# A gated linear attention and its MLP on one core: another order for the first phase, and products of gates with q and k taken from PSUM

## The chip, the core and the metric

One core of a Trainium2 chip. It has TensorE for matrix products (its loading of weights is listed as PEld), VectorE (DVE), ScalarE (ACT), GpSimd (POOL) and SyncE (SP), each with its own in-order instruction stream, on-chip memories SBUF and PSUM of 128 partitions, and DMA queues to HBM. TensorE writes to PSUM, and its results are read from there by VectorE and ScalarE. The metric is the device time of one execution in microseconds (us); lower is better.

## The reference

```python
# q, k, v, f_logit: (4, 8, 768, 48) float32
f = 1.0 / (1.0 + np.exp(-f_logit))
for t in range(S):                       # S = 768
    state = f[:, :, t, :, None] * state + np.einsum('bhd,bhe->bhde', k[:, :, t], v[:, :, t])
    y[:, :, t] = np.einsum('bhd,bhde->bhe', q[:, :, t], state)
x = y.transpose(0, 2, 1, 3).reshape(4, 768, 384)
mu, var = mean and variance of x over its last axis
xn = (x - mu) / np.sqrt(var + 1e-06) * g_ln
out = x + np.maximum(xn @ w_ch1, 0.0) @ w_ch2      # w_ch1 384 x 1536, w_ch2 1536 x 384
```

The two weight matrices arrive as 64-bit floats, which the kernel reads as pairs of 32-bit integers (`words`: `low` and `high`) and turns into 32-bit floats itself.

## The kernel before

**Units.** The 768 time steps are cut into 12 units of 64 steps, each for all four batches and eight heads (256 rows of the MLP). `attention(n)` (line 491) is a generator of four stages. Stage 1: `across` transposes the gates `f` on TensorE into single PSUM banks (tiles `tr`), ScalarE's sigmoid writes them to SBUF, and two scans on VectorE form the products of gates `after` (from each step to the unit's end) and `upto` (from the start), with small operations between them (`total`, its reciprocal, `least`). Stage 2: `k` and `q` are transposed, copied by ScalarE to `zk` and `zq` (line 531), and multiplied on POOL with `after` and `upto` to `kh` and `qh` (lines 534, 535). Stage 3: `kept` is the state times `total`; TensorE makes `py` from `qh` and `kept`, the scores `ps` from `kh` and `qh`, and `kp`, the transpose of `kh`; VectorE masks the scores (`sc`). Stage 4: `py` gets the scores' product with `v`; `pn` is the unit's contribution to the state, which VectorE adds; ScalarE copies `py` to `x`; mean and variance follow (`bn_stats`, `bn_aggr`, then `rstd` on POOL).

**MLP.** `normalize(n)` and `turn(n)` make `xn` and its transpose `xt` (tile `xp` in PSUM). `mlp(n)` (line 632) has 12 parts, each ending in a yield. Six are of `ph`: two of twelve strips of the hidden layer, from `xt` and `w1`, with ScalarE's ReLU into `h`. Six are of `po`: for each of two row groups three parts of four strips from `h` and `w2`, then VectorE's add `o` and two output DMAs. The matmul records of the trace count each 32-bit product twice, so a `ph` part has 12 and a `po` part 8 records.

**PSUM.** `ps1` (line 358) has four single banks, used in turn by `tr`, `kp`, `xp`, `ph` and `po`; `ps2` has two pairs for `py`, `ps` and `pn`.

**Order.** `manual_schedule` keeps the instructions of each engine in program order, and the program's order is written out in the last loops. Before the main loop three attentions run, with steps of the conversion of w1 between their stages; then the rest of w1, then `normalize(0)` and `turn(0)`. In the main loop the parts of `mlp(m)` alternate with the stages of `attention(m + 3)`, and in the first round three steps of the conversion of w2 follow each part.

**Conversion.** `weights` (line 421) takes each matrix in six pieces of 128 x 768 numbers, fetched one piece ahead. A piece goes through VectorE (exponent), POOL twice (limits, shift), VectorE (sign; fraction's bits), ScalarE (fraction to float), VectorE (low word), and a last product, on VectorE for w1, where the gain `g_ln` is multiplied in, on POOL for w2. Each step waits for the one before.

**Loads.** `load(n)` issues 16 DMAs of 96 KB on SyncE's queue, four for each of `f`, `q`, `k` and `v`. The tiles of `f`, `q` and `k` exist twice and are used in turn.

Of the kernel before, what the change touches and what calls it, by code (L numbers as in the profile page):

```python
# [8 lines left out]
FP32 = mybir.dt.float32  # L9
# [8 lines left out]
def general_path(tc, q, k, v, f_logit, w1, w2, ident, out):  # L18
# [228 lines left out]
    def mlp(n):  # L247
# [17 lines left out]
        for c in range(2):  # L265
            pt = one_bank(f"gxp{n}")[:, 0:KD * C].rearrange("p (m t) -> p m t", m=KD)
            for m in range(KD):
                nc.tensor.transpose(pt[:, m], xn[:, c, m * P:(m + 1) * P], ident)
            nc.scalar.copy(out=xt[:, :, c * C:(c + 1) * C], in_=pt)
# [33 lines left out]
def kernel(  # L303
# [38 lines left out]
    AHEAD = 3  # L342
# [4 lines left out]
    w2 = outer.tile([P, KF, DM], FP32)  # L347
    small = outer.tile([1, 1], I32)
# [5 lines left out]
    stage = fast.enter_context(tc.tile_pool(name="stage", bufs=2))  # L354
    work = fast.enter_context(tc.tile_pool(name="work", bufs=1))
    xs = fast.enter_context(tc.tile_pool(name="xs", bufs=AHEAD + 2))
# [20 lines left out]
    def load(n):  # L377
        if n >= NU:
            return
        vt = raws.tile([P, G, H, D], FP32, tag="rawv", name=f"v{n}")  # L380
        loaded[n] = [wide_heads[name, n % 2] for name in "fqk"] + [vt]
        for t, src in zip(loaded[n], (f_logit, q, k, v), strict=True):
            for b in range(B):
                nc.sync.dma_start(  # L384
                    out=t[(b % 2) * T:(b % 2 + 1) * T, b // 2, :, 0:D],
                    in_=src[b, :, n * T:(n + 1) * T, :].rearrange("h p d -> p h d"))

    load(0)
# [11 lines left out]
    nc.vector.memset(power, -0.5)  # L400

# [4 lines left out]
    for i in range(2):  # L406
        t = consts.tile([P, NS, E1], FP32, name=f"starts{i}")
        nc.vector.memset(t, 0.0)
        starts.append(t)
        t = consts.tile([P, NS * E1 + 1], FP32, name=f"gates{i}")  # L410
        nc.gpsimd.memset(t, 0.0)
        gates.append(t)
# [4 lines left out]
    gain = consts.tile([P, KD], FP32)  # L417
# [3 lines left out]
    def weights(dst, src, name, scaled):  # L421
        rows, cols = dst.shape[1], dst.shape[2]
        sv = src.rearrange("(c p) f -> p c f", p=P)
        r, w = (rows, PIECE // rows) if scaled else (PIECE // cols, cols)
        pieces = [(slice(i, i + r), slice(j, j + w))
                  for i in range(0, rows, r) for j in range(0, cols, w)]
        wide = src.dtype == mybir.dt.int64
        staged = []
        if wide:
            def fetch(i):  # L430
                ci, fi = pieces[i]
                words = stage.tile([P, r, 2 * w], I32, tag="words", name=f"{name}words{i}")
                nc.sync.dma_start(out=words, in_=sv[:, ci, fi].bitcast(I32))
                staged.append(words)
        else:
            def fetch(i):
                ci, fi = pieces[i]
                nc.sync.dma_start(out=dst[:, ci, fi], in_=sv[:, ci, fi])
        fetch(0)
        for i, (ci, fi) in enumerate(pieces):  # L440
            if i + 1 < len(pieces):
                fetch(i + 1)
            to = dst[:, ci, fi]
            if not wide:
                for c in range(r if scaled else 0):
                    nc.vector.tensor_scalar_mul(out=to[:, c], in0=to[:, c],
                                                scalar1=gain[:, c:c + 1])
                yield
                continue
            words = staged.pop(0)  # L450
            scale = stage.tile([P, r, w], I32, tag="scale", name=f"{name}scale{i}")
            frac = stage.tile([P, r, w], FP32, tag="frac", name=f"{name}frac{i}")
            wv = words.rearrange("p r (f two) -> p two r f", two=2)
            low, high = wv[:, 0].bitcast(U32), wv[:, 1]


            nc.vector.tensor_scalar(out=scale, in0=high, scalar1=20, scalar2=0x7FF,
                                    op0=ALU.logical_shift_right, op1=ALU.bitwise_and)
            nc.gpsimd.tensor_scalar(out=scale, in0=scale, scalar1=float(BIAS + 255),
                                    scalar2=float(BIAS), op0=ALU.min, op1=ALU.max)  # L460
            nc.gpsimd.tensor_scalar(out=scale, in0=scale, scalar1=float(-BIAS),
                                    scalar2=float(1 << 23), op0=ALU.add, op1=ALU.mult)
            yield
            nc.vector.scalar_tensor_tensor(out=scale, in0=high, scalar=-(1 << 31), in1=scale,  # L464
                                           op0=ALU.bitwise_and, op1=ALU.bitwise_or)

            nc.vector.tensor_scalar(out=high, in0=high, scalar1=0xFFFFF, scalar2=None,  # L467
                                    op0=ALU.bitwise_and)
            nc.scalar.activation(out=frac, in_=high, func=AF.Copy, bias=1.0, scale=2.0 ** -20)
            yield  # L470
            nc.vector.scalar_tensor_tensor(out=frac, in0=low, scalar=2.0 ** -52, in1=frac,
                                           op0=ALU.mult, op1=ALU.add)
            if scaled:
                for c in range(r):
                    nc.vector.scalar_tensor_tensor(  # L475
                        out=to[:, c], in0=frac[:, c], scalar=gain[:, c:c + 1],
                        in1=scale[:, c].bitcast(FP32), op0=ALU.mult, op1=ALU.mult)
            else:
                nc.gpsimd.tensor_tensor(out=to, in0=frac, in1=scale.bitcast(FP32), op=ALU.mult)  # L479
            yield  # L480

    pairs = [(g, a) for g in range(G) for a in range(NP)]
    x_of, xn_of, xt_of = {}, {}, {}
# [7 lines left out]
    def attention(n):  # L491

        fr, qr, kr, vt = loaded.pop(n)
        gt, st = gates[n % 2], starts[n % 2]
        gv = gt[:, 0:NS * E1].rearrange("p (s e) -> p s e", e=E1)


        zq = work.tile([P, NS, T], FP32, tag="zq", name=f"zq{n}")
        zk = work.tile([P, NS, T], FP32, tag="zk", name=f"zk{n}")

        def across(src, g):
            pt = one_bank(f"tr{n}")
# [5 lines left out]

        for g in range(G):
            pt = across(fr, g)  # L510
            nc.scalar.activation(out=gv[:, g * 8:(g + 1) * 8, 1:E1], in_=pt, func=AF.Sigmoid)  # L511

        after = work.tile([P, NS, E1], FP32, tag="after", bufs=2, name=f"after{n}")
        nc.vector.tensor_tensor_scan(  # L514
            out=after.rearrange("p s e -> p (s e)")[:, ::-1], data0=gt[:, NS * E1:0:-1],
            data1=ends.rearrange("p s e -> p (s e)")[:, ::-1], initial=0.0,
            op0=ALU.mult, op1=ALU.add)
        total = work.tile([P, NS], FP32, tag="total", bufs=2, name=f"total{n}")
        nc.vector.tensor_scalar_max(out=total, in0=after[:, :, 0], scalar1=1e-30)
        nc.vector.reciprocal(out=st[:, :, 0], in_=total)  # L520
        nc.vector.tensor_tensor(out=least, in0=least, in1=total, op=ALU.min)

        upto = work.tile([P, NS, E1], FP32, tag="upto", name=f"upto{n}")
        nc.vector.tensor_tensor_scan(  # L524
            out=upto.rearrange("p s e -> p (s e)"), data0=gt[:, 0:NS * E1],
            data1=st.rearrange("p s e -> p (s e)"), initial=0.0, op0=ALU.mult, op1=ALU.add)
        yield
        for src, dst in ((kr, zk), (qr, zq)):
            for g in range(G):
                pt = across(src, g)  # L530
                nc.scalar.copy(out=dst[:, g * 8:(g + 1) * 8], in_=pt)  # L531
        kh = work.tile([P, NS, T], FP32, tag="kh", bufs=2, name=f"kh{n}")
        qh = work.tile([P, NS, T], FP32, tag="qh", bufs=2, name=f"qh{n}")
        nc.gpsimd.tensor_tensor(out=kh, in0=zk, in1=after[:, :, 1:E1], op=ALU.mult)  # L534
        nc.gpsimd.tensor_tensor(out=qh, in0=zq, in1=upto[:, :, 1:E1], op=ALU.mult)  # L535
# [11 lines left out]
        if n:  # L547
            for e, (g, a) in enumerate(pairs):
# [8 lines left out]
        for e, (g, a) in enumerate(pairs):  # L557
# [19 lines left out]
        for across_ in range(2):  # L577
            for e, (g, a) in enumerate(pairs):
                for b in range(2):
# [4 lines left out]
                                     skip_group_check=True)  # L584
        if n < NU - 1:
# [10 lines left out]
            else:  # L596
                nc.vector.tensor_copy(out=state, in_=pnv)
        x = xs.tile([P, G, DM], FP32, tag="x", name=f"x{n}")
        x_of[n] = x
        nc.scalar.copy(out=x.rearrange("t g (a r d) -> t r (g a) d", r=2, d=D),  # L600
                       in_=py[:, :, 0:GA * D].rearrange("t r (e d) -> t r e d", d=D))
        stats = xs.tile([P, G, nc.vector.BN_STATS_DIM], FP32, tag="stats", name=f"stats{n}")
        mv = xs.tile([P, G, nc.vector.BN_AGGR_DIM], FP32, tag="mv", name=f"mv{n}")
        rstd = xs.tile([P, G], FP32, tag="rstd", name=f"rstd{n}")
        for g in range(G):
            nc.vector.bn_stats(out=stats[:, g], in_=x[:, g])
# [142 lines left out]
```

## Time and profile before

| | |
|---|---|
| Median of three runs | 618.77 us (618.66 to 619.63) |
| The profiled execution | 619.75 us, its span 618.0 us |
| TensorE busy | 506.4 us, 82% of the span |
| VectorE, ScalarE, POOL busy | 207.9, 123.2, 126.8 us |
| Mean granted TensorE clock | 0.907 of full speed |
| Read from and written to HBM | 28.31 and 4.72 MB |

A row of a group of instructions reads: line, engine, operation, result <- operands, shapes, count | busy us, mean ns of one | idle time of the engine before them, and what ended it. A row of the timeline: start, duration, engine, line, operation, operands, count, and in brackets the idle time before. A row of the windows: the stretch, its length, busy us and count for PE, PEld, DVE, ACT and POOL, then the granted clock, the DMA share and GB/s. A row of the chain of work that ended last: start, duration, engine, what. The slices divide the span in 40; a digit is the busy share in tenths. Matmuls are pipelined and their ends are modelled.

### The profile page before, as it was taken

To read this page: it belongs to the slowest core of one execution; us is meant where nothing else is said; L and a number is where in the kernel's file an instruction comes from. 1 tells how busy PE (TensorE), PEld (TensorE's weight loads), DVE (VectorE), ACT (ScalarE), POOL (GpSimd) and SP (SyncE) were. 2 spreads that over 40 slices of the span, in tenths; PEclk is the share of its full clock that TensorE was granted. 3 is DMA by queue.
4 is the path that set the end of the run, shared out by engine and by line. 5 is a ranking of instruction groups with operands and counts; after the bars stand their busy time and mean duration, and the time that the engine had idled before them with its cause. 6 is when DMAs were issued, how large, how long until landed. Compare 5 with 4: busy or idle time off the path is not lost.

```text
span 618.0 us, 10918 instructions
## 1 busy us (share of the span) xinstructions
PE 506.4 (82%) x4841; PEld 393.3 (64%) x4841; DVE 207.9 (34%) x265; ACT 123.2 (20%) x217; POOL 126.8 (21%) x95
## 2 busy tenths in 40 slices
PE   3061615647099999999999999999999999999995
PEld 2051605536077868778778687787876877777773
DVE  5078585563413335025233251243412511000100
ACT  3021121222112213113132131231311311111110
POOL 2044141255410403104013040040220400000000
PEclk9556666679579999999999999999999999999999
DMA  6968282182101403215024051150000000010101
GB/s 115 208 136 143 65 142 64 51 164 93 51 13 35 83 15 72 44 27 103 15 40 77 15 94 24 33 97 15 14 1 15 13 15 14 0 27 1 27 1 30
DMA packets 109702, 33.82 MB, mean 55 GB/s; under 512 B 102736, under 2 KB 105808, under 8 KB 109648
## 3 DMA queue, kind: packets, MB, share of 16 engines
q1 hardware_dynamic: 109648, 33.05, 26.2%
q8 instruction: 40, 0.66, 0.5%
q14 instruction: 14, 0.11, 0.1%
HBM read 28.31 MB, written 4.72 MB: 53 GB/s over the span
## 4 chain that ended last, share of the span: by engine, by line
PE 74%; DVE 12%; POOL 5%; SPq 3%; ACT 2%; issue 2%; DMA 1%; ACTq 0%
PE po L647 30%; PE ph L640 29%; PE py L581 3%; PE tr L504 3%; SPq L384 3%; PE py L551 2%; PE ps L561 2%; DVE w1scale L464 2%; PE kp L572 2%; PE pn L590 2%; PE xp L628 1%; DVE w1words L467 1%; POOL w L479 1%; DVE w L475 1%; DVE upto L524 1%
## 5 line engine op out<-in xcount | busy, mean ns | idle before, releaser
L640 PE MATMUL ph<-xt,w 128*128 128x256 f32 x864 | 197.2, 387 | 9.7 <-ACT zk L531 9.1
L647 PE MATMUL po<-w,h 128*128 128x384 f32 x576 | 194.6, 490 | 0.0
L640 PEld LDWEIGHTS ph<-xt,w 128*128 128x128 f32 x864 | 166.3, 194 | 35.6 <-ACT zk L531 9.4
L647 PEld LDWEIGHTS po<-w,h 128*128 128x128 f32 x576 | 107.8, 191 | 67.1 <-issue 1.1
L642 ACT ACTIVATE h<-ph 128x512 f32<-128x512 f32 x72 | 43.0, 597 | 168.4 <-PE ph L640 168.4
L652 DVE TENSOR_TENSOR o<-x,po 128x384 f32<-128x384 f32 x24 | 13.3, 555 | 175.1 <-PE po L647 175.1
L551 PE MATMUL py<-kept,qh 48*64 48x48 f32 x704 | 15.1, 243 | 57.4 <-DVE kept L541 57.4
L534 POOL TENSOR_TENSOR kh<-zk,after 128x1024 f32<-128x1024 f32 x12 | 38.8, 3237 | 101.0 <-ACT zk L531 101.0
L551 PEld LDWEIGHTS py<-kept,qh 48*64 48x64 f32 x704 | 13.7, 158 | 62.7 <-issue 62.7
L564 DVE TENSOR_TENSOR sc<-ps,causal 128x1024 f32<-128x1024 f32 x12 | 14.7, 1224 | 95.8 <-PE ps L561 95.8
L608 POOL TENSOR_SCALAR rstd<-mv 128x2 f32<-128x2 f32 x12 | 5.7, 473 | 189.5 <-DVE mv L607 189.5
L514 DVE TENSOR_TENSOR_SCAN after<-gates,ends 128x1040 f32<-128x1040 f32 x12 | 27.9, 2324 | 33.9 <-ACT gates L511 29.6
L561 PE MATMUL ps<-qh,kh 48*64 48x64 f32 x768 | 16.9, 250 | 21.4 <-POOL qh L535 21.4
L535 POOL TENSOR_TENSOR qh<-zq,upto 128x1024 f32<-128x1024 f32 x12 | 33.9, 2826 | 0.0
L561 PEld LDWEIGHTS ps<-qh,kh 48*64 48x64 f32 x768 | 15.7, 164 | 21.8 <-POOL qh L535 21.8
L581 PEld LDWEIGHTS py<-v,sc 64*64 64x64 f32 x768 | 24.9, 142 | 6.6 <-issue 5.1
L524 DVE TENSOR_TENSOR_SCAN upto<-gates,starts 128x1040 f32<-128x1040 f32 x12 | 27.9, 2325 | 0.6
L581 PE MATMUL py<-v,sc 64*64 64x48 f32 x768 | 26.4, 226 | 0.9 <-DVE sc L564 0.9
L629 ACT COPY xt<-xp 128x384 f32<-128x384 f32 x24 | 10.4, 482 | 82.4 <-PE xp L628 82.4
L541 DVE TENSOR_TENSOR kept<-state,total 128x768 f32<-128x768 f32 x11 | 25.8, 2346 | 0.0
L574 ACT COPY kt<-kp 128x512 f32<-128x512 f32 x24 | 13.2, 588 | 62.6 <-PE kp L572 62.6
L600 ACT COPY x<-py 128x768 f32<-128x768 f32 x12 | 9.5, 794 | 59.5 <-PE py L581 59.5
(63 smaller groups left out, 356.5 us busy)
## 6 DMA issues: line engine op xcount, KB each, us to landing
fraw<-in_f_logit_dram SPq DMA_DIRECT2D x48, 96.0 KB, 3.1
qraw<-in_q_dram SPq DMA_DIRECT2D x48, 96.0 KB, 3.2
kraw<-in_k_dram SPq DMA_DIRECT2D x48, 96.0 KB, 3.3
v<-in_v_dram SPq DMA_DIRECT2D x48, 96.0 KB, 3.2
w1words<-in_moe_w_ch_dram SPq DMA_DIRECT2D x6, 768.0 KB, 5.3
w2words<-in_moe_w_ch_dram SPq DMA_DIRECT2D x6, 768.0 KB, 4.4
out_dram<-o SPq DMA_DIRECT2D x48, 96.0 KB, 2.2
gain<-in_moe_g_ln_dram SPq DMA_DIRECT2D x1, 1.5 KB, 2.6
```

The lines of the kernel that those rows point to most:

```text
L384: nc.sync.dma_start(out=t[(b % 2) * T:(b % 2 + 1) * T, b // 2, :, 0:D], in_=src[b, :, n * T:(n + 1) * T, :].rearrange("h p d -> p h d"))
L514: nc.vector.tensor_tensor_scan(out=after.rearrange("p s e -> p (s e)")[:, ::-1], data0=gt[:, NS * E1:0:-1], data1=ends.rearrange("p s e -> ...
L524: nc.vector.tensor_tensor_scan(out=upto.rearrange("p s e -> p (s e)"), data0=gt[:, 0:NS * E1], data1=st.rearrange("p s e -> p (s e)"), ini ...
L534: nc.gpsimd.tensor_tensor(out=kh, in0=zk, in1=after[:, :, 1:E1], op=ALU.mult)
L535: nc.gpsimd.tensor_tensor(out=qh, in0=zq, in1=upto[:, :, 1:E1], op=ALU.mult)
L541: nc.vector.tensor_tensor(out=kept, in0=state, op=ALU.mult, in1=total.rearrange("p (e b) -> p b e", b=2).unsqueeze(3).broadcast_to([P, 2, ...
L551: nc.tensor.matmul(py[half(b), r, e * D:(e + 1) * D], lhsT=qh[head_rows(r), 2 * e + b], rhs=kept[head_rows(r), b, e], start=e == 0, stop=F ...
L561: nc.tensor.matmul(ps[half(b), r, e], lhsT=kh[head_rows(r), seg], rhs=qh[head_rows(r), seg], start=True, stop=True)
L581: nc.tensor.matmul(py[half(b), r, e * D:(e + 1) * D], lhsT=sc[half(b), r, e], rhs=vt[half(b), g, 2 * a + r], start=n == 0 and e == 0, stop ...
L640: nc.tensor.matmul(ph[:, j], lhsT=w1[:, m, (i + j) * P:(i + j + 1) * P], rhs=xt[:, m], start=m == 0, stop=m == KD - 1)
L642: nc.scalar.activation(out=h[:, i:i + 2], in_=ph, func=AF.Relu)
L647: nc.tensor.matmul(po, lhsT=h[:, i, g * P:(g + 1) * P], rhs=w2[:, i], start=i == 0, stop=i == KF - 1)
```

## The change

The first phase now runs attention 0 and attention 1 interleaved, with the first three pieces of w1 fetched behind loads 0 and 1. Then a piece is opened (`split`) and an earlier one finished (`join`) after every part of the next two MLP halves: the six `ph` parts of unit 0, each following the join of the piece of w1 that it needs, then the six `ph` parts of unit 1 beside the pieces of w2. The six `po` parts of both units follow, with `attention(2)` between them, and then a main loop in which `mlp(m)` goes with `attention(m + 1)` instead of `m + 3`. In it stage 3 moves from slot 6 to 5, stage 4 from 8 to 7, and the load from slot 1 to 2.

In a piece, the limits of the exponent are now a ReLU on ScalarE and one operation on POOL; the last product is on VectorE for both matrices. The gain is no longer in w1: ScalarE multiplies it into `xt`, in three operations of 128 columns for each row group, instead of one copy. In stage 2 the copies `zk` and `zq` are gone: VectorE multiplies the transposed tiles in PSUM with `after` and `upto`, in halves. For unit 0 the scans are done in halves too. Load 0 alternates between SyncE's and ScalarE's queues, and a small sigmoid runs ahead of the first. In stage 4 the copies to `x` (in halves) and the statistics come ahead of `pn`. The fallback `general_path` for very small gates takes the gain as an argument; it does not run on these inputs.

```diff
-            nc.scalar.copy(out=xt[:, :, g * P:(g + 1) * P], in_=pt)
+            for m in range(KD):
+                nc.scalar.mul(out=xt[:, m, g * P:(g + 1) * P], in_=pt[:, m],
+                              mul=gain[:, m:m + 1])
...
-    stage = fast.enter_context(tc.tile_pool(name="stage", bufs=2))
+    stage = fast.enter_context(tc.tile_pool(name="stage", bufs=3))
...
-    load(0)
+    load(0, (nc.sync, nc.scalar))
...
+    def split():
...
+        nc.vector.tensor_scalar(out=scale, in0=high, scalar1=20, scalar2=0x7FF,
+                                op0=ALU.logical_shift_right, op1=ALU.bitwise_and)
+        nc.vector.tensor_scalar(out=frac.bitcast(I32), in0=high, scalar1=0xFFFFF, scalar2=None,
+                                op0=ALU.bitwise_and)
+        nc.scalar.activation(out=scale, in_=scale, func=AF.Relu, bias=bias, scale=1.0)
+        nc.scalar.activation(out=frac, in_=frac.bitcast(I32), func=AF.Copy, bias=1.0,
+                             scale=2.0 ** -20)
+        nc.gpsimd.tensor_scalar(out=scale, in0=scale, scalar1=255.0, scalar2=float(1 << 23),
+                                op0=ALU.min, op1=ALU.mult)
...
+    def join():
...
+        nc.vector.scalar_tensor_tensor(out=frac, in0=low, scalar=2.0 ** -52, in1=frac,
+                                       op0=ALU.mult, op1=ALU.add)
+        nc.vector.scalar_tensor_tensor(out=scale, in0=high, scalar=-(1 << 31), in1=scale,
+                                       op0=ALU.bitwise_and, op1=ALU.bitwise_or)
+        nc.vector.tensor_tensor(out=to, in0=frac, in1=scale.bitcast(FP32), op=ALU.mult)
...
-        for src, dst in ((kr, zk), (qr, zq)):
+        for src, dst, by in ((kr, kh, after), (qr, qh, upto)):
             for g in range(G):
                 pt = across(src, g)
-                nc.scalar.copy(out=dst[:, g * 8:(g + 1) * 8], in_=pt)
...
-        nc.gpsimd.tensor_tensor(out=kh, in0=zk, in1=after[:, :, 1:E1], op=ALU.mult)
-        nc.gpsimd.tensor_tensor(out=qh, in0=zq, in1=upto[:, :, 1:E1], op=ALU.mult)
+                segs = slice(g * HS, (g + 1) * HS)
+                nc.vector.tensor_tensor(out=dst[:, segs], in0=pt, in1=by[:, segs, 1:E1],
+                                        op=ALU.mult)
...
+    for _ in range(3):
+        fetch()
+    first, second = attention(0), attention(1)
+    for stages in (first, first, first, second, first, second):
         next(stages)
...
     normalize(0)
     turn(0)
...
+    split()
+    next(second)
+    split()
+    join()
+    fetch()
+    mlps = mlp(0), None
+    for part in range(6):
+        next(mlps[0])
+        if part == 0:
+            next(second)
+        elif part == 1:
+            normalize(1)
+        elif part == 2:
+            turn(1)
+        split()
+        join()
+        fetch()
+    mlps = mlps[0], mlp(1)
+    for part in range(6):
+        next(mlps[1])
+        split()
+        join()
+        fetch()
+        if part == 3:
+            load(2, (nc.sync,))
...
+    third = attention(2)
+    for part in range(12):
+        next(mlps[part // 6])
+        if part in (1, 2, 5, 7):
+            next(third)
...
+    for m in range(2, NU):
+        n = m + 1
         stages = attention(n) if n < NU else iter(())
         parts = mlp(m)
         for slot in range(12):
             next(parts)
...
+            if slot in (0, 1, 5, 7):
                 next(stages, None)
...
+            elif slot == 2:
+                load(n + 1, (nc.sync,))
```

244 lines of the change are left out of this document (105 added, 139 removed).

## The prediction

> **What bounds the kernel now.** I read the page's slices first, then the same in two windows split at 176 us, then the chain of work that ended last, in order of time.
>
> ```profile
> PE   3061615647099999999999999999999999999995
> ...
> 0.00:176.00 176.00, 70.86 (x1046) 61.59 (x1047) 93.58 (x116) 34.42 (x55) 63.43 (x61) 0.69 0.51 108
> 176.00:612.00 436.00, 435.51 (x3797) 331.68 (x3795) 114.25 (x149) 88.80 (x163) 63.32 (x34) 1.00 0.17 33
> ...
> 23.25 5.39 DMA w1words<-in_moe_w_ch_dram
> ...
> 170.72 1.96 PE py L551 x64
> ...
> 176.31 6.26 PE po L647 x16
> 182.57 1.93 PE py L581 x61
> ...
> 194.10 2.59 PE ph L640 x12
> ...
> 234.58 2.59 PE ph L640 x12
> ...
> 517.02 15.54 PE ph L640 x72
> ...
> 548.70 10.36 PE ph L640 x48
> ...
> 596.03 15.49 PE po L647 x48
> ...
> 611.54 0.56 DVE L652 TENSOR_TENSOR o<-x,po 128x384 f32<-128x384 f32 x1 [7.18 <-PE po L647]
> ```
>
> Slices and windows show two regimes end to end. From 176 us on TensorE is busy 435.5 of 436 us at a granted clock of 1.00: only less work or less waiting moves that part. Before 176 us it is busy 71 us at 0.69; weight conversion, on three engines in turn, sets the pace. So the question is when TensorE becomes dense, how much work is left then, and whether it stays dense.
>
> The work comes from the chain. A unit with attention beside it takes 234.58 - 194.10 = 40.48 us, one without 548.70 - 517.02 = 31.68; attention is the difference, 8.8; a unit's `po` is 15.5; a part of `ph` (one yield of `mlp`, a sixth of the unit's) is 2.59. The end, from 611.5 to the span's 618.0, is 6.5.
>
> **The change, part by part.** *Work left.* When all weights are joined in the new order, TensorE has done attention 0 and 1, all twelve `ph` parts of units 0 and 1 and, since `po` follows its pieces, two of the three parts of the first `po` half (5.2). Left are ten units of 31.68, ten attentions of 8.8, 31.0 of `po` for units 0 and 1, less 5.2, 0.9 (gate transposes of unit 2) and 0.9 (unit 11 has no `pn`): 428.8 us. Before, 435 were left at 176. The gain is a start that comes earlier; call it E.
>
> *The first two units.* These rows stand for what goes.
>
> ```profile
> 0.79 2.79 SPq L384 DMA_DIRECT2D fraw<-in_f_logit_dram  x4
> ...
> 7.49 1.09 ACT L511 ACTIVATE gates<-tr 128x512 f32<-128x512 f32 x2
> ...
> 31.01 2.16 POOL L534 TENSOR_TENSOR kh<-zk,after 128x1024 f32<-128x1024 f32 x1
> 31.08 2.90 DVE L464 SCALAR_TENSOR_TENSOR w1scale<-w1words,w1scale 128x768 int32<-128x768 int32 x1 [1.86 <-POOL w1scale L461]
> ...
> 36.06 1.99 PE L561 MATMUL ps<-qh,kh 48*64 48x64 f32 x64 [21.39 <-POOL qh L535]
> ...
> 115.17 5.41 PE L640 MATMUL ph<-xt,w 128*128 128x256 f32 x12 [0.57 <-ACT xt L629]
> ```
>
> The scores of unit 0 waited until 36 us because `kh` stood on POOL behind the first piece of w1, which landed at 23.25 + 5.39 = 28.6. That queueing goes. The durations for the new order:
>
> ```profile
> L464 DVE SCALAR_TENSOR_TENSOR w2scale<-w2words,w2scale 128x768 int32<-128x768 int32 x6 | 5.8, 959 | 22.0 <-POOL w2scale L461 22.0
> L471 DVE SCALAR_TENSOR_TENSOR w2frac<-w2words,w2frac 128x768 f32<-128x768 uint32 x6 | 5.8, 958 | 9.8 <-ACT w2frac L469 9.8
> L467 DVE TENSOR_SCALAR w2words<-w2words 128x768 int32<-128x768 int32 x6 | 3.4, 562 | 0.2
> L595 DVE TENSOR_TENSOR state<-kept,pn 128x768 f32<-128x768 f32 x10 | 9.5, 953 | 19.4 <-PE pn L590 19.4
> L564 DVE TENSOR_TENSOR sc<-ps,causal 128x1024 f32<-128x1024 f32 x12 | 14.7, 1224 | 95.8 <-PE ps L561 95.8
> L606 DVE BATCH_NORM_STATS2 stats<-x 128x6 f32<-128x384 f32 x24 | 13.0, 541 | 3.9 <-ACT x L600 3.9
> L618 DVE TENSOR_SCALAR xn<-x,mv,rstd 128x384 f32<-128x384 f32 x24 | 10.1, 465 | 0.0
> L469 ACT ACTIVATE w2frac<-w2words 128x768 f32<-128x768 int32 x6 | 5.4, 895 | 31.5 <-issue 18.4 <-DVE w2words L467 13.1
> L461 POOL TENSOR_SCALAR w2scale<-w2scale 128x768 int32<-128x768 int32 x6 | 5.0, 831 | 0.5
> L629 ACT COPY xt<-xp 128x384 f32<-128x384 f32 x24 | 10.4, 482 | 82.4 <-PE xp L628 82.4
> L642 ACT ACTIVATE h<-ph 128x512 f32<-128x512 f32 x72 | 43.0, 597 | 168.4 <-PE ph L640 168.4
> w2words<-in_moe_w_ch_dram SPq DMA_DIRECT2D x6, 768.0 KB, 4.4
> ```
>
> The new product of gates and `k` or `q` from PSUM has no row. It lies between an `o` add (0.56, 384 columns) and `sc` (1.22, 1024 columns), both from PSUM; I take 0.69 for 512 columns, 2.75 for the four of a unit.
>
> VectorE's chain, in program order. The first half of the gates is ready at 8.1 as now: ScalarE issues half of load 0, eight DMAs at 0.7 each, and is done at 6.2, ahead of the table load that precedes the first sigmoid anyway. Half scans for both halves, together two of 2.32 and two gaps of 0.6 (from `after` to `upto` in the unit quoted below), end at 14.0; four products 16.8; `ps` and `kp` on a cold TensorE (2.0 each), then transposes and sigmoids (1.0 each) of unit 1 bring 22.9; its scans (5.2) 28.1; statistics (two of 0.54 with their aggregates, 1.5) and state (1.0) of unit 0 30.6; products 33.3; normalize (two of 0.46) 34.2; split 0 (two of 0.56) 35.3; `kept`, as large as the state add, 36.3; `py` and `ps` cold (1.96 + 1.99) and `sc` 41.6; split 1 and join 0 (0.96 + 0.96 + 0.95 = 2.87) 45.6. The first three pieces are fetched behind load 1, no later than today's 28.6, so they are there.
>
> Then comes a trap: stage 4 of unit 1 follows the first `ph` part. VectorE waits for that part (2.6 warm, 5.4 cold, rows above), `py` (1.93), two `x` copies (0.48 each, as the `xt` copies of that size), then does statistics and state (1.7), split 2 and join 1 (4.0): join 1 ends at 57 or 60. I take 60. The remaining ten pieces cost 3.98 on VectorE each (1.1 + 2.87), 39.8, plus normalize 0.9 and 1.9 where ScalarE makes six small scalings of `xt` before join 4's fraction: 102.5. The other loops of an iteration are shorter: `ph`, ReLU, scale and fraction on ScalarE (2.9 + 0.6 + 1.8), then the join, span two iterations in about 8.2, and a fetch of 4.4 has about 5. (On SyncE's queue each fetch waits for the join that frees its buffer; behind it stand the later fetches and load 2, which unit 2 needs only near 100 us.) TensorE's own `ph` parts and 5.2 of `po` nearly fill this time too.
>
> POOL's 0.83 per piece lies beside VectorE at best. Beside POOL's `kh` the 0.96 us instruction took 2.90 (rows at 31.01 and 31.08). So a piece costs 0 to 0.83 more, E = 99.7 (warm, free) to 111 (cold, always blocked). I take 103, near the free end, since VectorE waits in iterations where POOL can run.
>
> The Trainium skill, SBUF — State Buffer, "Who interferes with whom", calls this port an exclusive lock between GpSimd reads and a VectorE instruction with two SBUF inputs. By it every overlap costs the full 0.83, so E would be nearer 111 and the time 574; the row at 31.08 agrees that the blocked one waits the other out.
>
> *Steady state: a new wait.* In every later unit `k` and `q` stay in PSUM until VectorE has finished both scans.
>
> ```profile
> 237.01 1.04 PE L504 MATMUL tr<-ident,fraw 128*128 128x128 f32 x8
> 237.76 1.08 ACT L511 ACTIVATE gates<-tr 128x512 f32<-128x512 f32 x2
> 238.87 2.32 DVE L514 TENSOR_TENSOR_SCAN after<-gates,ends 128x1040 f32<-128x1040 f32 x1 [3.70 <-ACT gates L511]
> ...
> 241.80 2.32 DVE L524 TENSOR_TENSOR_SCAN upto<-gates,starts 128x1040 f32<-128x1040 f32 x1
> ...
> 242.22 10.53 PE L640 MATMUL ph<-xt,w 128*128 128x256 f32 x48
> ...
> 134.31 1.06 ACT L531 COPY zk<-tr 128x512 f32<-128x512 f32 x2
> 134.93 13.53 PE L640 MATMUL ph<-xt,w 128*128 128x256 f32 x48 [9.14 <-ACT zk L531]
> ```
>
> There are four single banks (line 358). The four `tr` tiles of `k` and `q` take all four; the next `ph` needs one back. The rows at 134 show exactly that: `ph` waits for ScalarE's copy of the first `k` half. Today that copy is done in time; afterwards the bank comes back with the first product, behind `upto`. In the unit shown: `upto` ends at 244.1, product 244.8, semaphore, `ph` at 244.9 instead of 242.15. TensorE waits 2.75 us; all behind it (`ph`, ReLU, `po`) waits too. Nine units (n = 3 to 11) give 24.8. Unit 2 stands beside `po`: its scans begin at E, the `o` add and the first product follow at 5.2 and 5.8 later, while TensorE has a `po` part (2.6) and 1.3 of transposes to do: about 2.3. If the products took 0.56 or 1.22 each, the nine waits would be 2.6 to 3.3.
>
> *What costs nothing.* The six `xt` scalings take 0.25 each (482 for 384 columns, 597 for 512: 115 per 128), 1.6 instead of 0.9 behind a `po` burst of 2.58; without that cover, 0.7 a unit. POOL's products and ScalarE's copies leave engines with slack. Loads are issued most of a unit ahead. Statistics before the state add delay the state, needed a unit later.
>
> **The sum.** 103 + 428.8 + 2.3 + 24.8 + 6.5 = 565.4 span. The profiled execution took 619.75 and its span 618.0; the median shown is 618.77, 0.8 above the span. Forecast: **566 us**.
>
> **The rivals.**
> - *No bank wait.* The `ph` finds a bank, or scans end sooner: 566 - 25 = 541. The rows at 134.93 speak against it. 0.05.
> - *The state products wait for `x`.* `pn` now comes behind the `x` copies in the program; if it got `py`'s banks rather than `ps`'s, it would wait for two copies and a semaphore, about 1.2 a unit: 577. Nothing today shows `pn` waiting; the pool would have to prefer the bank freed last. 0.08.
> - *The clock falls in each bank wait.* After 9.14 us idle 48 records took 13.53 instead of 10.36: 3.2 lost, at most 29 over nine units: up to 595. For it: a wait recurs every unit. Against: 2.75 is far shorter than 9.14. 0.10. The Trainium skill, TensorE: Matmul & The Clock Gate, "HAM oscillation — how this bites in real kernels", puts the limit near 3.4 us idle, by which nothing is lost, while its section "A second HAM failure mode: psum-queue depth-cycling" tells of oscillation from micro-idling between bursts, by which part of the 29 would be. No row here has an idle of 2 to 4 us in a dense stretch, so the trace decides neither.
> - *The skew does not take.* Pieces keep today's pace of about 7.5 us
>
> ```profile
> 154.78 2.04 POOL L479 TENSOR_TENSOR w<-w2frac,w2scale 128x768 f32<-128x768 f32 x1 [3.64 <-DVE w2frac L471]
> 162.29 2.04 POOL L479 TENSOR_TENSOR w<-w2frac,w2scale 128x768 f32<-128x768 f32 x1 [3.64 <-DVE w2frac L471]
> ```
>
> because ScalarE, in order behind each ReLU, delivers late: ten pieces at 3.5 more, 601. Against: the fraction is issued an iteration before its join. 0.04.
> - *Slower than before.* The clock stays at half after each wait through the unit's last four `ph` parts: 10.4 more a unit, 93 in all, 659. It decides from 5.8 us a unit ((618.8 - 566) / 9). The 13.53 speaks against it. 0.03.
>
> **How the numbers follow.** The forecast has 0.70. Its own bounds, E from 99.7 to 111 and waits of 2.6 to 3.3, give 561 to 579; prologue terms worked out from cold rows can be some us shorter. The range 552 to 588 takes these, the `pn` case and half of the clock case, some 0.8. Faster by over 0.2% (about what a measurement of this kernel can tell from no change): 0.96; within: 0.01; slower: 0.03.
>
> **What would show it.** TensorE dense from about 103 us in the slices; the last join near 100; a wait of `ph` for VectorE's product of 2.7 us in nine units in the table of waits; the unit period 43.2 instead of 40.5 where attention runs; `pn` without a wait; clock 1.00 after 103. A unit period of 40.5 would refute the bank argument; an E beyond 111 the sum of the first phase.

## The result, and the profile after

The changed kernel takes 586.87 us (median, 585.79 to 587.1), the kernel before in the same runs 619.2: a ratio of 0.947 (95% interval 0.946 to 0.949). The forecast was 566, its range 552 to 588. The profiled execution took 586.91 us, its span 585.2.

Slices and windows of the changed kernel; the two windows are a unit in which the clock fell and one in which it held.

```profile
PE   4645779789899899989989989989989989989996
PEclk9957779989989989989989999989989989999999
...
195.28:240.05 44.77, 42.44 (x415) 32.61 (x415) 13.72 (x20) 8.15 (x18) 0.93 (x2) 0.96 0.24 46
329.49:372.57 43.08, 40.74 (x415) 31.45 (x415) 13.73 (x20) 8.16 (x18) 0.93 (x2) 1.00 0.24 47
```

TensorE was dense from 176 us before; it is dense from about 111 now. But where its digits were all nines they have eights in them, in a rhythm, and the clock's digits too: something recurs in each unit. The waits of TensorE name it.

```profile
PE ph L656 <- DVE kh L546: 21.1, 9, 2.4
PE ph L656 <- DVE w L481: 16.9, 4, 6.2
...
PE tr L505 <- DVE o L668: 2.8, 1, 2.8
...
PE py L563 <- DVE kept L553: 1.5, 1, 1.5
```

Nine waits of 2.34 us for VectorE's first product: the bank wait. Here is the unit of the first window in the timeline. Below it, from the chain of work that ended last, stand the `po` parts behind the wait of unit 2, and the last four `ph` parts of the first window's unit and of the second's:

```profile
199.51 2.32 DVE L518 TENSOR_TENSOR_SCAN after<-gates,ends 128x1040 f32<-128x1040 f32 x1 [3.64 <-ACT gates L533]
...
202.05 1.04 PE L505 MATMUL tr<-ident,qraw 128*128 128x128 f32 x8
...
202.37 2.33 DVE L527 TENSOR_TENSOR_SCAN upto<-gates,starts 128x1040 f32<-128x1040 f32 x1
...
204.68 1.28 DVE L546 TENSOR_TENSOR kh<-tr,after 128x512 f32<-128x512 f32 x2
205.42 5.84 PE L656 MATMUL ph<-xt,w 128*128 128x256 f32 x18 [2.33 <-DVE kh L546]
```

```profile
116.90 9.66 PE po L663 x24
...
205.42 12.31 PE ph L656 x48
...
339.63 10.63 PE ph L656 x48
```

The eight transposes of `q` end at 203.09 and hold the last of the four single banks; `ph` starts at 205.42, one product behind the second scan. Its 48 records then take 12.31 us where they took 10.36 before. In two of the nine units they take 10.63. Small windows in that stretch show the clock:

```profile
199.00:205.40 6.40, 4.08 (x27) 3.52 (x25) 5.78 (x7) 1.08 (x2) 0.00 (x0) 1.00 0.76 141
205.40:207.40 2.00, 1.98 (x6) 1.66 (x7) 2.00 (x4) 0.00 (x0) 0.00 (x0) 0.66 0.81 145
207.40:209.40 2.00, 2.00 (x6) 1.53 (x6) 0.62 (x1) 0.00 (x0) 0.00 (x0) 0.50 0.83 148
209.40:211.40 2.00, 2.00 (x11) 1.77 (x10) 0.00 (x0) 0.60 (x1) 0.00 (x0) 0.99 0.16 28
```

It is granted in full during the wait, and falls to half only when TensorE is back at work, for some 3 us. That costs 12.31 - 10.63 = 1.7 us in each of seven units. The 0.27 by which 10.63 exceeds the 10.36 of before is not the clock's: in the second window it was 1.00 throughout. It stays unexplained.

**Where the prediction and the span part.** Predicted 565.4, measured 585.2, 19.8 more:

| Term | Predicted | Measured | Difference |
|---|---|---|---|
| E, the end of the last join | 103 | 110.6 | +7.6 |
| Nine bank waits | 24.8 | 21.1 | -3.7 |
| `ph` behind the nine waits | 0 | seven units at 12.2 to 12.3, two at 10.63, against 10.36 | +14.1, of which the clock 11.6 |
| Wait in unit 2 | 2.3 | 2.8 | +0.5 |
| `po` behind that wait | 0 | 24 records at 9.66, against 7.94 later in the unit | +1.7 |
| Wait of `py` for `kept` in unit 2 | 0 | 1.5 | +1.5 |
| End | 6.5 | 5.0 | -1.5 |
| Not accounted for | | | -0.4 |

The `po` parts behind the wait of unit 2 are a tenth case of the falling clock: it was 0.50 from 117.75 to 120.25.

Within E, the second join ended at 59.2, as worked out (60). It is the ten pieces behind it that took 51.4 instead of 42.5. The chain of the changed kernel there:

```profile
64.40 0.83 ACT w_768scale L465
65.30 2.79 POOL w_768scale L468
...
70.21 5.47 PE ph L656 x12
76.31 0.83 ACT w_1280scale L465
77.21 2.78 POOL w_1280scale L468
```

This is the loop over two pieces that the prediction put at 8.2 and took for shorter than VectorE's own: from 64.40 to 76.31 it is 11.9. POOL's one operation takes 2.79 us, where each of the two that it replaces took 0.83, and the `ph` part takes 5.47 at a granted clock of 0.50 (from 70.20 to 75.70), behind a wait of TensorE for the join.

### The profile page after: what moved, and what is told of

Its sections match the earlier page's. It is cut to its first block, busy times and chain, and to the rows that moved or that the text cites. A ratio compares the mean times of both kernels' runs of the same rounds, so it can differ in the third digit from the quotient of the medians.

```text
span 585.2 us, 10892 instructions
## 1 busy us (share of the span) xinstructions
PE 518.4 (89%) x4841; PEld 396.7 (68%) x4841; DVE 217.5 (37%) x312; ACT 118.4 (20%) x242; POOL 52.9 (9%) x53
## 4 chain that ended last, share of the span: by engine, by line
PE 72%; DVE 19%; ACT 3%; issue 1%; POOL 1%; DMA 1%; DVEq 0%; ACTq 0%
PE po L663 31%; PE ph L656 28%; DVE upto L527 5%; DVE after L518 5%; PE py L593 4%; PE ps L573 2%; PE py L563 2%; PE kp L584 2%; ACT gates L533 2%; DVE w L481 2%; PE pn L616 2%; PE xp L641 1%; DVE kh L546 1%; DVE w_0scale L479 1%; DMA qraw<-in_q_dram 1%
## 5 line engine op out<-in xcount | busy, mean ns | idle before, releaser
L656 PE MATMUL ph<-xt,w 128*128 128x256 f32 x864 | 213.2, 408 | 38.0 <-DVE kh L546 21.1
L606 DVE BATCH_NORM_STATS2 stats<-x 128x6 f32<-128x384 f32 x24 | 13.0, 543 | 81.8 <-ACT x L604 81.8
L518 DVE TENSOR_TENSOR_SCAN after<-gates,ends 128x1040 f32<-128x1040 f32 (+1 forms) x13 | 28.0, 2156 | 41.0 <-ACT gates L533 41.0
L643 ACT ACTIVATE xt<-xp,gain 128x128 f32<-128x128 f32 x72 | 19.9, 376 | 91.6 <-PE xp L641 91.6
L527 DVE TENSOR_TENSOR_SCAN upto<-gates,starts 128x1040 f32<-128x1040 f32 (+1 forms) x13 | 28.1, 2158 | 0.4
L593 PE MATMUL py<-v,sc 64*64 64x48 f32 x768 | 24.8, 219 | 0.0
L604 ACT COPY x<-py 128x384 f32<-128x384 f32 x24 | 10.3, 482 | 67.5 <-PE py L593 67.5
L468 POOL TENSOR_SCALAR w_0scale<-w_0scale 128x768 int32<-128x768 int32 x7 | 22.2, 3171 | 14.7 <-ACT w_0scale L465 14.7
L505 PE MATMUL tr<-ident,fraw 128*128 128x128 f32 x96 | 13.6, 285 | 5.1 <-DMA fraw<-in_f_logit_dram 5.1
L505 PE MATMUL tr<-ident,qraw 128*128 128x128 f32 x96 | 13.6, 286 | 3.6 <-DVE o L668 2.8
L505 PEld LDWEIGHTS tr<-ident,fraw 128*128 128x128 f32 x96 | 11.8, 148 | 6.7 <-POOL causal L398 4.4
```

The costliest lines, as they stand in the source:

```text
L468: nc.gpsimd.tensor_scalar(out=scale, in0=scale, scalar1=255.0, scalar2=float(1 << 23), op0=ALU.min, op1=ALU.mult)
L505: nc.tensor.transpose(pt[:, a * P:(a + 1) * P], src[:, g, 2 * a:2 * a + 2].rearrange("p h e -> p (h e)"), ident)
L518: nc.vector.tensor_tensor_scan(out=after.rearrange(flat)[:, c0:c1][:, ::-1], data0=gt[:, c0 + 1:c1 + 1][:, ::-1], data1=ends.rearrange(fla ...
L527: nc.vector.tensor_tensor_scan(out=upto.rearrange(flat)[:, c0:c1], data0=gt[:, c0:c1], data1=st.rearrange(flat)[:, c0:c1], initial=0.0, op ...
L593: nc.tensor.matmul(py[half(b), r, e * D:(e + 1) * D], lhsT=sc[half(b), r, e], rhs=vt[half(b), g, 2 * a + r], start=n == 0 and e == 0, stop ...
L643: nc.scalar.mul(out=xt[:, m, g * P:(g + 1) * P], in_=pt[:, m], mul=gain[:, m:m + 1])
```

## The experiments

Two theories. *Steady state:* the bank wait costs its 2.34 us nine times, and what follows it, the fall of the clock above all, another 14 in all; rival: the clock falls for a reason of its own. *First phase:* E is late by POOL's slow operation; rivals: the place of stage 4 of unit 1, ScalarE, load 0.

**1. Let VectorE have its time (late).** Stage 2 goes one slot later, so that a `ph` part stands between the scans' start and the transposes that fill the banks.

```diff
-            if slot in (0, 1, 5, 7):
+            if slot in (0, 2, 5, 7):
...
-            elif slot == 2:
+            elif slot == 3:
                 load(n + 1, (nc.sync,))
```

> Stage 2 of units 3 to 11 in slot 2 instead of 1, the load in slot 3 instead of 2; nothing else. Theory (the four single banks, all held by k and q until VectorE's scans are done): the scans are finished when the transposes come, so the wait of ph for the product, 2.33 us in each of nine units, falls below 0.2, and with it the slow stretch behind it (12.31 instead of 10.36 us for the last four ph parts in seven units); the unit period goes from 44.8 to 40.5 us, the time from 587 to about 552. Rival 1 (the waiting only moves, to the next ph part or to kept and ps): period above 42, time above 565. Rival 2 (the slow stretch has nothing to do with the wait but comes with the load's DMAs, which run at a share of 0.8 at that moment): the wait goes and the slow stretch stays, 566.

553.44 us, 0.894 of before (0.891 to 0.897): 33.4 below the changed kernel. No `ph` waits for `kh` in the table of waits, and the chain has a unit of 40.50 us, with the three parts behind stage 2 at full speed:

```profile
191.15 2.59 PE ph L656 x12
...
231.65 2.59 PE ph L656 x12
...
242.04 7.78 PE ph L656 x36
```

The wait (21.1) and the slower `ph` behind it (14.1) are 35.2 by the table above; 33.4 came back. So both go with the wait. (The wait in unit 2 stays, and its 24 records of `po` take 9.66 here too.)

**2. Fill the wait, wholly (fill5) and in part (fill2).** These tell the clock from the wait: TensorE is kept busy in the gap, and `ph` comes no sooner.

```diff
         yield
+        if n > 2:
+            spare = two_banks(f"spare{n}")
+            for _ in range(5):
+                nc.tensor.matmul(spare[:, 0, 0:W], lhsT=w1[:, 0, 0:P], rhs=w1[:, 1, 0:W],
+                                 start=True, stop=True)
```

The lines stand at the end of stage 2; fill2 has `range(2)`.

> Five products of weights with weights, read by nobody, behind the q transposes of units 3 to 11, in a free pair of banks: 2.2 us of TensorE work in the place where it waits 2.33 us. Theory (the idle stretch makes the clock fall): ph starts no earlier, but its last four parts take about 10.4 us in all nine units, period 42.8, time about 573. Rival (the slow stretch comes with the load's DMAs or with the reading of other banks): still 12.3 us in most units, time 587.

> As fill5 with two products instead of five: 0.86 us of TensorE work in the wait, so about 1.5 us of idle stay. Theory (the idle share of some span of time decides, and 2.33 us is near its edge, since two of nine units escaped): with 1.5 us all nine units keep the clock, period 43.1, time about 576. Rival (any idle of over a us makes the clock fall): 12.3 us in most units, 587.

fill5: 576.27 us, 0.930 (0.927 to 0.932), 10.6 less than the changed kernel for five products of no use. Its waits and its chain:

```profile
PE ph L661 <- DVE kh L546: 1.6, 9, 0.2
```

```profile
195.18 2.60 PE ph L661 x12
...
205.32 10.63 PE ph L661 x48
...
238.27 2.60 PE ph L661 x12
```

All nine units have 10.63, and a period of 43.09, that of the changed kernel's unit in which the clock held (43.08). fill2, in a single run, took 576.12 us. Its gap is longer:

```profile
PE ph L661 <- DVE kh L546: 13.3, 9, 1.5
```

Still all nine have 10.63. So the idle time brings the clock down: in these units 1.5 us never did, 2.34 did in seven of nine. But the length of one gap doesn't settle it. In nolimit (experiment 4) TensorE has two waits in unit 2:

```profile
112.03 0.66 PE L505 MATMUL tr<-ident,qraw 128*128 128x128 f32 x4 [2.59 <-DVE o L668]
...
122.16 1.15 PE L563 MATMUL py<-kept,qh 48*64 48x48 f32 x64 [1.51 <-DVE kept L553]
```

```profile
124.60:126.60 2.00, 2.00 (x9) 1.82 (x9) 1.07 (x1) 0.86 (x2) 0.00 (x0) 0.50 0.81 146
```

The clock is 1.00 all the way from the wait of 2.59 to the one of 1.51, and falls some 2 us behind the shorter one; oneq and late_dve have the same picture there. What decides which wait is followed by a fall stays open.

**3. Undo the product alone (oldprod), and make it alone (befprod).** In the changed kernel ScalarE copies the transposed tiles out of PSUM again, and POOL multiplies; the kernel before gets the products from PSUM and nothing else.

```diff
-        for src, dst, by in ((kr, kh, after), (qr, qh, upto)):
+        for src, dst in ((kr, kh), (qr, qh)):
             for g in range(G):
                 pt = across(src, g)
-                segs = slice(g * HS, (g + 1) * HS)
-                nc.vector.tensor_tensor(out=dst[:, segs], in0=pt, in1=by[:, segs, 1:E1],
-                                        op=ALU.mult)
+                nc.scalar.copy(out=dst[:, g * HS:(g + 1) * HS], in_=pt)
+        nc.gpsimd.tensor_tensor(out=kh, in0=kh, in1=after[:, :, 1:E1], op=ALU.mult)
+        nc.gpsimd.tensor_tensor(out=qh, in0=qh, in1=upto[:, :, 1:E1], op=ALU.mult)
```

> The product of gates with q and k undone in the changed kernel: ScalarE copies the transposed tiles, POOL multiplies them in place. Theory (the new product is what holds the banks): no wait of ph in the steady state, unit period 40.5 us, but some 2 to 3 us more in the chain of each of the first two units, time about 556. Rival (the wait comes from the new order of slots, not from the product): period 44.8, time about 592.

> Only the product edit, put into the kernel before: VectorE multiplies k and q in PSUM, ScalarE's copies and POOL's products gone, all else as before. Theory (the product holds the four banks until the scans are done; the first phase is bound by conversion): ph of units 3 to 11 waits about 2.3 us nine times and most waits cost 1.7 to 1.95 us of half clock behind them, 35 us; unit 0 leaves POOL's queue, which gives back some 5 to 15 us ahead of 176 us; time about 640 to 650, slower than before. Rival (POOL's and ScalarE's relief is what the product brings; the wait comes from the new slots): period 40.5, time below 619.

oldprod: 559.2 us (552.59 to 559.87), 0.899 (0.893 to 0.905): 27.7 faster than with the product on VectorE (three of its four runs lie between 558.9 and 559.9, one at 552.6, which isn't explained). Its last join ends at 115.4, 4.8 later; the first is as much later already (50.1 against 45.3), with one of POOL's products in the chain ahead of it. A window over one unit shows TensorE without a gap:

```profile
157.96:198.44 40.48, 40.48 (x416) 31.43 (x415) 13.28 (x16) 10.10 (x22) 7.59 (x4) 1.00 0.27 50
```

befprod: 637.27 us, 1.030 (1.028 to 1.031), slower than before. The expectation named 640 to 650: 35 for the waits and the clock behind them, less 5 to 15 for an earlier start. The waits and the chain:

```profile
PE ph L637 <- DVE kh L531: 28.8, 9, 10.3
```

```profile
179.84 2.60 PE ph L637 x12
189.95 12.31 PE ph L637 x48
224.58 2.60 PE ph L637 x12
```

The unit period is 44.74 instead of 40.48, over eight units 34.1 lost; but unit 1's first `ph` part stands at 179.84 where it stood at 194.10 (quoted in the prediction), 14.3 earlier, near the far end of what was expected. In the chain of before, two of VectorE's conversion instructions take 2.92 and 2.41 (at 31.08 and 34.02) beside POOL's two products, and the like at 57.79 and 88.94; in befprod these are gone from the chain. How much of the 14.3 that makes was not tested apart. (The ninth wait, 10.3, lies ahead of 179 us, where before had its 9.14.) One of the eight kept its clock (1.7): 34.1 - 1.7 - 14.3 = 18.1, and the span grew by 18.0 (618.0 to 636.0). So the product edit helps the first phase and costs more later: in the changed kernel it takes back nearly half of what the new order brings.

**4. POOL's operation.** nolimit keeps one operation there but makes it an add of 0 and the multiplication; the upper limit of the exponent is left out.

```diff
-        nc.gpsimd.tensor_scalar(out=scale, in0=scale, scalar1=255.0, scalar2=float(1 << 23),
-                                op0=ALU.min, op1=ALU.mult)
+        nc.gpsimd.tensor_scalar(out=scale, in0=scale, scalar1=0.0, scalar2=float(1 << 23),
+                                op0=ALU.add, op1=ALU.mult)
```

> POOL's one operation per piece is add 0 and multiply instead of limit and multiply; the upper limit of the exponent is left out. Theory (the pair of operations is slow on POOL): 2.78 us falls to 0.83 as with the two operations of before, the last join ends about 6 to 8 us earlier than 110.6, time about 580. Rival 1 (the input, written by ScalarE, or the single pass makes it slow): 2.78 stays, 587. Rival 2 (POOL is faster but TensorE's cold ph parts of 4.6 us set the pace): join 11 at 107 or later, time 584.

578.91 us (577.58 to 581.19), 0.934 (0.931 to 0.936). The groups of that line, first of the changed kernel, then of this one (its fastest instance is 0.83):

```profile
L468 POOL TENSOR_SCALAR w_0scale<-w_0scale 128x768 int32<-128x768 int32 x7 | 22.2, 3171 | 14.7 <-ACT w_0scale L465 14.7
```

```profile
L468 POOL TENSOR_SCALAR w_0scale<-w_0scale 128x768 int32<-128x768 int32 x7 | 7.3, 1047 | 23.0 <-ACT w_0scale L465 23.0
```

Same shape, types and place; only the first of the two functions and its constant differ. Why `min` is slow there isn't known. The last join ends at 106.2: 4.4 of the 7.6, where the expectation named 6 to 8. In the profiled execution, 5.7 shorter in its span than the changed kernel's, three units kept their clock instead of two, which is another 1.7. The median is 8.0 lower; how many units kept theirs in the runs without a profile isn't known.

**5. Other homes for the limit, on top of the later stage 2 (late_two, late_dve).** late_two goes back to POOL's two operations of before and drops the ReLU on ScalarE; late_dve gives the `min` and multiplication to VectorE at the start of `join`, and POOL nothing.

```diff
@@ late_two, split()
-        nc.scalar.activation(out=scale, in_=scale, func=AF.Relu, bias=bias, scale=1.0)
...
+        nc.gpsimd.tensor_scalar(out=scale, in0=scale, scalar1=float(BIAS + 255),
+                                scalar2=float(BIAS), op0=ALU.min, op1=ALU.max)
+        nc.gpsimd.tensor_scalar(out=scale, in0=scale, scalar1=float(-BIAS),
+                                scalar2=float(1 << 23), op0=ALU.add, op1=ALU.mult)
@@ late_dve, first line of join()
+        nc.vector.tensor_scalar(out=scale, in0=scale, scalar1=255.0, scalar2=float(1 << 23),
+                                op0=ALU.min, op1=ALU.mult)
```

> As late, and the limits of the exponent on POOL in the two operations of before (limit from both sides, then add and multiply), ScalarE's ReLU on the exponent gone. Theory (the slow pair on POOL and its wait for ScalarE behind ph stretch the two-piece loop): two operations of 0.83 us, started by VectorE directly; the last join ends near 105 instead of 110.7, time about 548. Rival (POOL's port use of 1.66 per piece blocks VectorE as long as it saves): join 11 near 110, time 553.

> As late, and the operation that was slow on POOL is done by VectorE at the start of join; POOL has no part in a piece. Theory: 0.56 us more on VectorE per piece, no wait for POOL and no blocked port; pieces of 4.5 us where VectorE sets the pace, last join near 106, time about 549. Rival (the cold ph parts and ScalarE behind them set the pace of the first six pieces): no gain there and a loss of 0.56 on the others, 553 or more.

late_two: 551.32 us, 0.891 (0.889 to 0.892), 2.1 below late; the last join ends at 110.0 instead of late's 110.7. That is the rival's number. Its timeline over one piece:

```profile
92.83 1.07 POOL L467 TENSOR_SCALAR w_0scale<-w_0scale 128x768 int32<-128x768 int32 x1 [2.47 <-DVE w_0scale L461]
93.13 1.58 DVE L478 SCALAR_TENSOR_TENSOR w_0frac<-w_0words,w_0frac 128x768 f32<-128x768 uint32 x1
...
93.98 1.42 POOL L469 TENSOR_SCALAR w_0scale<-w_0scale 128x768 int32<-128x768 int32 x1
94.63 1.57 DVE L480 SCALAR_TENSOR_TENSOR w_0scale<-w_0words,w_0scale 128x768 int32<-128x768 int32 x1
96.24 0.96 DVE L482 TENSOR_TENSOR w<-w_0frac,w_0scale 128x768 f32<-128x768 f32 x1
```

Both engines hold each other up: VectorE's instructions take 1.58 instead of 0.96, POOL's 1.07 and 1.42 instead of 0.83. A piece takes 5.05 (96.24 less the row of the same line at 91.19). That is the cost which the prediction put down to a shared port and bounded by POOL's own time, 0.83 for one operation; here, with two (1.66), VectorE loses 1.23 (1.58 and 1.57, less twice 0.96).

late_dve, with 0.47 us more work on VectorE per piece and no POOL: **544.34 us**, 0.879 (0.878 to 0.881), 9.1 below late. From the third piece on `ph` parts take 2.83, warm, and pieces 4.3 to 4.9. Its scan behind the last join:

```profile
102.94 2.33 DVE L518 TENSOR_TENSOR_SCAN after<-gates,ends 128x1040 f32<-128x1040 f32 x1 [0.76 <-ACT gates L533]
```

The last join ends at 102.2, 8.5 earlier than late's and 4 earlier than the expectation's theory. So POOL's part makes up the 7.6: the slow operation 4.4, by nolimit, and the rest by what VectorE and the loop lose with an operation on POOL. How the rest divides was not measured.

**6. Stage 4 of unit 1 (late_dve_s4).** late_dve with that stage behind the next split, join and fetch instead of in front of them.

```diff
         next(mlps[0])
-        if part == 0:
-            next(second)
-        elif part == 1:
+        if part == 1:
             normalize(1)
...
         fetch()
+        if part == 0:
+            next(second)
```

> This is the kernel of late_dve with one call moved: stage 4 of unit 1 (state products, copies of x, statistics, new state) is taken from its place directly behind the first ph part and put behind the split, the join and the fetch of that part. In the changed kernel, and in late_dve, VectorE's second join waits behind that stage for the ph part, for py, for two copies and for the state (it starts at 45.4 and ends at 59.2, where its own work is about 4 and that of the stage 1.7). Theory that this place costs the first phase time: the second join ends near 50, the stage runs beside the next ph part, and the last join ends 4 to 8 us earlier than the 102.9 of late_dve: 537 to 540. Rival: the pieces behind it are paced by TensorE's cold ph parts and ScalarE, and the stage only stands in their way one iteration later: last join at 102 to 103, 544 as late_dve.

542.82 us, 0.877 (0.876 to 0.879); the interval overlaps late_dve's. Its second and third product and its last scan, from the timelines of two stretches:

```profile
48.38 0.96 DVE L481 TENSOR_TENSOR w<-w_256frac,w_256scale 128x768 f32<-128x768 f32 x1
...
58.99 0.96 DVE L481 TENSOR_TENSOR w<-w_512frac,w_512scale 128x768 f32<-128x768 f32 x1
...
102.03 2.32 DVE L518 TENSOR_TENSOR_SCAN after<-gates,ends 128x1040 f32<-128x1040 f32 x1
```

The second join ends at 49.3 instead of 58.9, and nothing comes of it: the third ends at 59.95 instead of 63.9, and the last where it did. The rival is right. What the prediction called a trap is real as a wait, but its removal only moves it; the median's 1.5 us, if they are any, aren't explained.

**7. Load 0 on one queue (oneq).** The changed kernel with `load(0, (nc.sync,))`.

> The changed kernel with load 0 issued on SyncE's queue alone, as in the kernel before. The prediction had ScalarE done with its eight issues at 6.2; its trace has it held until 8.3, the table load at 8.3 and the first sigmoid at 9.7. Theory that the second queue brought nothing or cost a little: ScalarE is free for its table load from the start, the gates' tiles come on the one queue by about 8, the first sigmoid is no later than 9.7, and since the joins up to 45 follow from it, the time is 584 to 587.5. Rival: one queue issues sixteen DMAs of f, k and q in turn, k and q land 2 to 5 us later, the first phase ends as much later: 589 to 592.

584.47 us, 0.944 (0.941 to 0.947): 2.4 less than the changed kernel, with intervals that just overlap (0.946 to 0.949 there). ScalarE and the first scan, in the changed kernel and here:

```profile
6.44 1.84 ACTq L386 DMA_DIRECT2D v<-in_v_dram  x2
...
8.32 1.28 ACT L407 ACT_TABLE_LOAD   x1 [8.32 <-DMA qraw<-in_q_dram]
...
10.33 1.24 DVE L518 TENSOR_TENSOR_SCAN after<-gates,ends 128x520 f32<-128x520 f32 x1 [5.93 <-ACT gates L533]
```

```profile
0.79 1.28 ACT L407 ACT_TABLE_LOAD   x1 [0.79 <-PEq L764]
...
6.84 1.24 DVE L518 TENSOR_TENSOR_SCAN after<-gates,ends 128x520 f32<-128x520 f32 x1 [2.43 <-ACT gates L533]
```

With the issues gone from ScalarE its table load is over at 2.1, and the first scan runs 3.5 us earlier, 1.8 of which are left at the last join (108.8). The spans of the two profiled executions differ by 3.2: these 1.8, and 1.7 since three units kept their clock here instead of two. By these traces the second queue for load 0 cost 1.8 us.

## Why the prediction was right, and where it was off

- **Faster, because TensorE is dense earlier.** Right. 176 became 110.6; the order, with the product edit taken out, gives 559.2. The size was met at its edge: 586.87 is 1.1 under the end of the range and above the 561 to 579 of the forecast's own bounds. It lies inside because half of the clock's price was put into the range.
- **The bank wait.** Right in mechanism, place and count. Its size was 2.34 instead of 2.75: the prediction let `ph` be ready at 242.15, which stands in no row. The `q` transposes of that unit (`241.34 1.04 PE L504 MATMUL tr<-ident,qraw 128*128 128x128 f32 x8`) end at 242.38, 3.51 behind the start of the first scan; in the changed kernel they end 3.58 behind it, and `ph` starts 5.91 behind it instead of 6.03. The product, which had no row, took 0.68 against 0.69.
- **The clock.** This is the larger of the two terms that were off. It was a rival at 0.10, with 2.75 us called "far shorter than 9.14", the one idle time behind which it had read off a price. The runs show that 2.34 is enough in most units (seven of nine here, six of nine in oneq and in nolimit, seven of eight in befprod), and late and fill5 that the clock holds in those units where the gap is gone. A single row at 9.14 said nothing of where between 0 and 9.14 the effect sets in; that was the weak argument. Its price, 29 at most and half of it in the range, was sound: some 13 came, 11.6 in the nine units and 1.7 in unit 2. The Trainium skill, TensorE: Matmul & The Clock Gate, "HAM oscillation — how this bites in real kernels", puts the limit near 3.4 us idle; by that all nine units would have kept their clock, and here 2.34 was too long in seven.
- **Slower than before, by a clock at half through four parts.** Refuted in size: the fall lasts 3 us and costs 1.7 a unit, under the 5.8 from which it would have decided.
- **E.** The first join (45.3 against 45.6) and the second (59.2 against 60) came as worked out, in part by luck: ScalarE was done with load 0 at 8.3 instead of 6.2 and the first scan began at 10.33 instead of 8.1, and shorter steps behind it made up for that. The step that failed is the sentence that the other loops of an iteration are shorter, 8.2 for two pieces. It took POOL's new operation at the 0.83 of L461, an add and a multiplication; a `min` and a multiplication take 2.79. And it took `ph` at 2.9, at full clock, while TensorE waits for the joins, and where the chain passes through `ph` a part takes 4.5 to 5.5. With the operation off POOL (late_dve) the last join ends at 102.2, near the 103, but that is another sum: VectorE has 0.47 more a piece there. In unit 2 the prediction also left out the wait of `py` for `kept` (1.5).
- **`pn` waiting for `x`.** Refuted: no such row in the table of waits.
- **The skew.** It takes: a join follows its split by an iteration, and the ten pieces take 5.1 us each on average instead of the 7.5 of before.

## What to carry to other kernels

A tile that stays in PSUM until a slow consumer is ready holds its bank, and the next matmul behind it pays; look for the first product that needs that bank, and put work of the dense engine between (one slot later brought 33 us here). A short recurring gap in a dense stretch is to be priced with the clock that follows it, from a gap of its own length and not from a long one, and even then as a chance. An operation that looks like its neighbours (same engine, shape and types, another function) is a new operation, and its price a bound until a row shows it.

## What the runs showed of the hardware that was not expected

- On POOL, `min` then multiplication on 128x768 int32 took 2.77 us at least, `add` then multiplication 0.83, `min` then `max` 0.83.
- The granted clock falls after the gap, and not in it: 0.5 us into the next work in the unit shown, 1 us in unit 2 of the changed kernel, near 2 us in unit 2 of nolimit. It is back some 3 us later. A wait of 1.51 us was followed by a fall where one of 2.59 was not.
- VectorE isn't held for the whole of POOL's long operation. In the changed kernel's timeline:

```profile
100.63 2.92 POOL L468 TENSOR_SCALAR w_0scale<-w_0scale 128x768 int32<-128x768 int32 x1 [1.50 <-ACT w_0scale L465]
100.83 1.58 DVE L479 SCALAR_TENSOR_TENSOR w_0scale<-w_0words,w_0scale 128x768 int32<-128x768 int32 x1
...
102.45 0.96 DVE L481 TENSOR_TENSOR w<-w_0frac,w_0scale 128x768 f32<-128x768 f32 x1
```

VectorE is done at 102.41, POOL at 103.55, and VectorE's next product, from SBUF too, takes its own 0.96 beside the same operation. The Trainium skill, SBUF — State Buffer, "Who interferes with whom", calls the shared port an exclusive lock. Held for the whole of POOL's operation, VectorE would have ended 0.96 behind POOL, near 104.5; here it lost 0.6. In late_two it took the same 1.58 and 1.57 beside POOL's operations of 1.07 and 1.42.
